# A causal convolution in front of a feed-forward layer: smaller TensorE tiles for the convolution, at another place in the block, and none of it on GpSimd

## The chip, the core and the metric

The kernel runs on one core of a Trainium2 chip. The metric is the time of one execution on the device in microseconds: the kernel before took 464.19 us (median of three runs, 463.25 to 464.36). The profile is one further execution of it, with a span of 462.7 us from the first to the last instruction; the granted TensorE clock was 1.000 throughout.

## What is computed

The input `x` has 8 sequences of 4160 tokens with 192 channels in float32. The 192 channels are 8 heads of 24. A softmax over `weight` (8 heads x 7 taps) gives seven convolution weights per head, and each channel is convolved causally along its sequence with the seven weights of its head. The 33,280 convolved tokens then pass through a maxout layer of width 768 with three branches, and a product that brings them back to 192 channels.

```python
out = np.einsum('hk,bskhg->bshg', w, x_unf)      # w = softmax(weight), 7 taps
h = np.maximum(np.maximum(x @ w1, x @ w2), x @ w3)
return (h @ w_out)
```

The kernel uses an identity to save a third of the maxout's work on the vector side. With `a = x(w1-w3)` and `b = x(w2-w3)`, the maximum of the three is `x w3 + max(relu(a), b)`. So only two products are made per token, the hidden value `max(relu(a), b)` goes through `w_out`, and the part `x w3 w_out` is one small product with the 192x192 matrix `m = w3 w_out`, worked out once at the start.

## The kernel before

**Blocks.** The tokens are cut into 65 blocks of 512. A loop over `t` runs the first product of block `t` (`l1`, L499) interleaved with the second product of block `t-1` (`st2`, L551). For each of the six groups `j` of 128 hidden features, `l1(t, j)` makes three pairs of matmuls with 512 columns each, and one call of `st2` makes five pairs with 192 columns each.

**Two lanes.** Every one of these matmuls contracts over 64 rows only. One half of the pair uses the lower 64 rows of the TensorE array (lane 0: the tiles `lp` and `po0`) and the other the upper 64 rows (lane 1: `lq`, `po1`), so the two run side by side. Both lanes need the convolved tokens in their own partitions, so the convolved block (`yd`) is kept twice, with the halves exchanged. After `l1`, ScalarE takes the ReLU of `lp` (L503) and VectorE the maximum with `lq` (L504).

**Three ways to convolve.** Blocks 0 to 3 are convolved at the start with the channels as outputs (`conv_dense`, L415). Twelve later blocks, those in `qpos`, are convolved on GpSimd: `load_q`, `cast_q`, a transposing DMA (`turn_q`), and then `tap_q`, seven multiplications (L229) with six additions (L237, L240). The other 49 are convolved on TensorE by `conv` (L397): block 4 alone, then 24 pairs of blocks. For this a block is cut into eight stretches of 64 tokens. Each is loaded with its six predecessors, which gives 70 rows, and multiplied with a banded 70x64 matrix that holds the seven taps of a head. One call of `conv` has 16 matmuls (8 heads, 2 column halves of the array), with 192 columns for a pair of blocks. The result `G` lies in four PSUM banks, two evacuated by ScalarE and two by VectorE (`evac`, L443).

**From `G` to `yd`.** A transposing DMA (`turn`, L454) brings the channels to the partitions, one DMA per block; two more DMAs (`double`, L462) write the exchanged copy. These, the loads of `x` (`load_x`, L144) and the stores of the result (`store`, L580) are all issued by SyncE's queue in the order of the program, and an issue that has to wait keeps those behind it waiting. GpSimd casts the loaded `x` to float16 (`cast_x`, L176).

**Where the convolution stands.** `conv` for block `t+3` and its successor is called right after `l1(t, 0)`, behind one single matmul of `st2` for lane 0 (`first_half_only`). The tiles of `l1` alternate between two banks for each lane (pools `psp` and `psq`), and `G` and the `po` tiles share four more (`psw`):

```python
l1(t, 0)
if t > 2 and u < NB:
    st2(t - 1, 0, NJ, True)
conv(u, PQ if t == 2 else WPWQ)
```

The order on each engine is that of the program text; nothing is reordered by a scheduler.

Of the kernel before, what the change touches and what calls it, by code (L numbers as in the profile page):

```python
# [14 lines left out]
P = 128  # L15
# [12 lines left out]
def kernel(  # L28
# [42 lines left out]
    qpos = [q for q in range(11, NB - 3, EVERY)] + [NB - 1]  # L71
# [23 lines left out]
    NR = NBLK // HALF  # L95

    def rows_of(t):
        rows = [(b, S + o) for (b, S, N, off) in blocks[t] for o in range(0, N, HALF)]
        assert len(rows) == NR
        return rows  # L100
# [4 lines left out]
    xfp = ctx.enter_context(tc.tile_pool(name="xfp", bufs=6))  # L105
# [5 lines left out]
    ydp = ctx.enter_context(tc.tile_pool(name="ydp", bufs=6))  # L111
# [9 lines left out]
    xin = {}  # L121

    def load_x(t, eng=nc.sync):
        if not 0 <= t < NB or t in qset:
            return
        pool, tag = (xfp, "xf") if t > 1 else ((xap, "xa"), (xbp, "xb"))[t]
        xf = pool.tile([P, NR, D], FP32, tag=tag, name=f"xf_{t}")
        if t < NDENSE:
            todo = [(0, c[3], c[1] * SEQ + c[2]) for c in chunks_of[t]]
        else:  # L130
            todo = [(PAD, HALF, b * SEQ) if s == 0 else (0, HALF + PAD, b * SEQ + s - PAD)
                    for b, s in rows_of(t)]
# [3 lines left out]
        while i < n:  # L136
            k = i
            while k + 1 < n and todo[k + 1][:2] == todo[i][:2] and row[k + 1] - row[k] == row[i + 1] - row[i]:
                k += 1
            step = row[i + 1] - row[i] if k > i else 0  # L140
            p0, rlen = todo[i][:2]
            src = bass.AP(tensor=x.tensor, offset=row[i] * D,
                          ap=[[D, rlen], [step * D, k - i + 1], [1, D]])
            eng.dma_start(out=xf[p0:p0 + rlen, i:k + 1, :], in_=src)  # L144
            if parts and parts[-1][0] == rlen:
                parts[-1] = (rlen, parts[-1][1], k + 1)
            else:
                parts.append((rlen, i, k + 1))
# [16 lines left out]
    def cast_x(t):  # L165
        if not 0 <= t < NB or t in qset:
            return
        xf, p0, _ = xin.pop(t)
        t0, u, nu = place(t)
        if u == 0:  # L170
            x16s[t0] = x16p.tile([P, NHEAD, 2, nu, NR // 2, GRP], FP16, tag="x16", name=f"x16_{t0}")
        if p0:
            nc.gpsimd.memset(xf[0:p0, 0, :], 0.0)
        K = HALF + PAD
        for c in range(2):
            nc.gpsimd.tensor_copy(out=x16s[t0][0:K, :, c, u, :, :].rearrange("p h r c -> p r h c"),  # L176
                                  in_=xf[0:K, c:NR:2, :].rearrange("p r (h c) -> p r h c", c=GRP))


# [41 lines left out]
    def tap_q(q, k):  # L221
# [17 lines left out]
        yd = dense[q] = ydp.tile([P, 2, NCH // 2, P], FP16, tag="yd", name=f"yd_{q}")  # L239
# [41 lines left out]
    for t in range(2, 7):  # L281
        load_x(t)

# [3 lines left out]
    nc.gpsimd.tensor_copy(out=ident16[:], in_=ident[:])  # L287
    idle = const.tile([P, NBLK], FP16)
# [25 lines left out]
    for v in range(2):  # L314
        nc.gpsimd.memset(xz[1][v][:], 0.0)
    wcol16 = const.tile([P, 3, KW], FP16)
# [70 lines left out]
    def conv(t, pools):  # L387
# [4 lines left out]
        per = NHEAD // n  # L392
        w = nu * (NR // 2) * GRP
        G = [pool.tile([P, per, w], FP32, tag=tag, name=f"G{i}_{t}") for i, (pool, tag) in enumerate(pools)]
        for h in range(NHEAD):
            for c in range(2):
                nc.tensor.matmul(  # L397
                    G[h // per][HALF * c:HALF * (c + 1), h % per, :],
                    lhsT=band[0:HALF + PAD, h, PAD:HALF + PAD],
                    rhs=x16s[t0][0:HALF + PAD, h, c, :, :, :].rearrange("p u r c -> p (u r c)"),  # L400
                    start=True, stop=True, tile_position=(0, HALF * c))
        slots[t0] = ysp.tile([P, nu, NR // 2, D], FP16, tag="ys", name=f"ys_{t}")
# [35 lines left out]
    def evac(t, i, copy=nc.scalar.copy):  # L438
# [3 lines left out]
        per = NHEAD // len(G)  # L442
        copy(out=slots[t][:, :, :, GRP * per * i:GRP * per * (i + 1)].rearrange(  # L443
# [3 lines left out]
    def turn(t):  # L447


        if t >= NB or t in qset:  # L450
            return
        t0, u, nu = place(t)
        yd = dense[t] = ydp.tile([P, 2, NCH // 2, P], FP16, tag="yd", name=f"yd_{t}")
        nc.sync.dma_start_transpose(out=yd[:, 0, :, :],  # L454
                                    in_=slots[t0][:, u, :, :].rearrange("p r d -> p (r d)"))

    def double(t):

        if NDENSE <= t < NB:
            yd = dense[t]  # L460
            for i in range(2):
                nc.sync.dma_start(out=yd[HALF * i:HALF * (i + 1), 1, :, :],  # L462
                                  in_=yd[HALF * (1 - i):HALF * (2 - i), 0, :, :])

    def spot(t, i, c, r):
# [3 lines left out]
        else:  # L469
            own, k = (NC * r + c) % 2, (NC * r + c) // 2  # L470
        return k + (0 if own == i else NCH // 2)

    def y_all(t, i, c):
        row = slice(HALF * i, HALF * (i + 1))
        if t < NDENSE:
            return dense[t][row, c, :]
        a = dense[t][row, 0, 0, :]
# [5 lines left out]
    def y_tok(t, i, c, s):  # L483
        row = slice(HALF * i, HALF * (i + 1))
        if t < NDENSE:
            return dense[t][row, c, P * s:P * (s + 1)]
        k = spot(t, i, c, s)
        return dense[t][row, k // 6, k % 6, :]

    def l1(t, j, pools=((psp, "p"), (psq, "q"))):  # L490


        N = blkN[t]
        ps = [pool.tile([P, NBLK], FP32, tag=tag, name=f"l{tag}{i}_{t}_{j}")
              for i, (pool, tag) in enumerate(pools)]
        for c in range(NC):
            for i in range(2):
                row = slice(HALF * i, HALF * (i + 1))
                nc.tensor.matmul(ps[i][:, 0:N], lhsT=wd[row, c, P * j:P * (j + 1)],  # L499
                                 rhs=y_all(t, i, c),  # L500
# [254 lines left out]
```

## Time and profile before

| | |
|---|---|
| time, median of 3 | 464.19 us |
| span of the profiled execution | 462.7 us |
| TensorE matmul busy | 454.4 us, 98% of the span |
| VectorE, ScalarE, GpSimd busy | 77%, 68%, 76% |
| bytes moved by DMA | 80.77 MB, mean 175 GB/s |
| `conv` calls on TensorE, matmuls in them | 25, 400 |
| blocks convolved on GpSimd | 12 |

The page of a profile begins with the busy time of each engine. Since matmuls are pipelined, a TensorE that is busy 98% of the time only says that some matmul was in flight, not that the array worked at its peak. What a stage costs is better read from the distance between the starts of its instructions in the timeline. The chain of waits is followed back from the last instruction; where it stays on one engine for hundreds of microseconds, that engine's queue set the end. In the rows for groups of instructions, `out<-in` gives the tiles, then come shape and count, the busy time, the mean duration of one, and the idle time of the engine just before them with what ended it. `64*128` means 64 rows and 128 columns of the array.

### The profile page before, as it was taken

What the parts mean: (1) busy time and instruction counts of PE and PEld (TensorE: products, weight loads), DVE (VectorE), ACT (ScalarE), POOL (GpSimd) and SP (SyncE); (2) the same over time, 40 slices, a digit from 0 to 9 for tenths busy, and PEclk for the clock granted to TensorE, in tenths of its full rate; (3) what the DMA queues carried; (4) which work ended last, traced back from release to release, by engine and by line L of the source; (5) the groups of instructions that cost most, each with busy time, mean ns of one, the idle gap of its engine ahead of it and who ended that gap; (6) DMA issues with size and microseconds to landing.
All of it is one profiled execution on the core that took longest, in us unless ns stands there. A gap on an engine that the chain in (4) does not pass through costs nothing.

```text
span 462.7 us, 17259 instructions
## 1 busy us (share of the span) xinstructions
PE 454.4 (98%) x6969; PEld 367.9 (80%) x6969; DVE 354.1 (77%) x595; ACT 314.3 (68%) x597; POOL 352.6 (76%) x501
## 2 busy tenths in 40 slices
PE   8999999999999999999999999999999999999997
PEld 4576788977877887888888888888888888888886
DVE  6777777777778787777878777777777777777775
ACT  5766566667676666767667676676767676676664
POOL 5753289999988978978967978978957969979500
PEclk9999999999999999999999999999999999999999
DMA  8959999999869878787789697698598797884423
GB/s 190 222 127 198 177 209 179 192 209 224 192 130 231 170 155 211 175 181 183 166 175 198 157 211 165 157 213 198 132 210 179 164 224 176 144 191 92 100 70 103
DMA packets 137527, 80.77 MB, mean 175 GB/s; under 512 B 58294, under 2 KB 137368, under 8 KB 137448
## 3 DMA queue, kind: packets, MB, share of 16 engines
q1 hardware_dynamic: 137176, 79.18, 79.1%
q8 instruction: 54, 0.88, 0.9%
q0 software_dynamic: 112, 0.39, 0.3%
q14 instruction: 25, 0.20, 0.2%
q10 hardware_dynamic: 160, 0.10, 0.1%
HBM read 29.85 MB, written 25.56 MB: 120 GB/s over the span
## 4 chain that ended last, share of the span: by engine, by line
PE 89%; POOL 5%; DMA 4%; issue 1%; DVE 0%; ACT 0%; POOLq 0%; DVEq 0%; SPq 0%
PE lq L499 35%; PE po L551 33%; PE lp L499 14%; PE G L397 4%; POOL tap L237 2%; POOL tap L229 2%; DMA yd<-ys 1%; PE idle L294 1%; DMA xt<-xq 1%; DMA yd<-yd 1%; PE D L415 1%; POOL x L176 1%; DMA xt<-xt 1%; PE lw L499 0%; PE band_cols L335 0%
## 5 line engine op out<-in xcount | busy, mean ns | idle before, releaser
L504 DVE TENSOR_TENSOR h<-r,lq 128x512 f16<-128x512 f16 x386 | 264.7, 686 | 99.5 <-ACT r L503 99.4
L503 ACT ACTIVATE r<-lp 128x512 f16<-128x512 f32 x386 | 230.5, 597 | 134.7 <-PE lp L499 123.8
L499 PE MATMUL lp<-yd,wd 64*128 64x512 f16 x1158 | 312.3, 376 | 2.2 <-DMA yd<-yd 1.6
L499 PE MATMUL lq<-yd,wd 64*128 64x512 f16 x1158 | 312.3, 376 | 0.3 <-DVE yd L431 0.3
L551 PE MATMUL po<-wo,h 64*128 64x192 f16 x3120 | 263.8, 243 | 0.7 <-issue 0.7
L551 PEld LDWEIGHTS <-h 64*128 64x128 f16 x3120 | 209.2, 94 | 22.2 <-issue 0.9
L499 PEld LDWEIGHTS <-wd 64*128 64x128 f16 x2340 | 160.9, 94 | 39.4 <-DMA yd<-yd 2.1
L176 POOL CAST x<-xf 70x768 f16<-70x768 f32 x98 | 77.8, 822 | 60.6 <-DMA xf<-in_x_dram 54.0
L229 POOL TENSOR_SCALAR tap<-xt,wcol 128x256 f32<-128x256 f16 x252 | 116.1, 478 | 3.9 <-DMA xt<-xt 3.3
L237 POOL TENSOR_TENSOR tap<-tap,tap 128x768 f32<-128x768 f32 x60 | 108.6, 1809 | 5.0
L551 PE MATMUL po<-m,yd 64*128 64x192 f16 x780 | 109.4, 243 | 0.0
L561 DVE TENSOR_TENSOR o<-a,po 128x384 f32<-128x384 f32 (+1 forms) x132 | 71.4, 541 | 1.2 <-ACT a L560 1.2
L551 PEld LDWEIGHTS <-yd 64*128 64x128 f16 x780 | 61.9, 94 | 11.8
L560 ACT COPY a<-po 128x384 f32<-128x384 f32 (+1 forms) x132 | 62.3, 473 | 3.0 <-PE po L551 3.0
L443 DVE CAST ys<-G 128x384 f16<-128x384 f32 x49 | 24.9, 550 | 0.6 <-PE G L397 0.6
L397 PEld LDWEIGHTS <-band 70*64 70x64 f16 x400 | 15.8, 109 | 9.9 <-PE lp L499 9.0
L240 POOL TENSOR_TENSOR yd<-tap,tap 128x768 f16<-128x768 f32 x12 | 21.8, 1814 | 1.0
L397 PE MATMUL G<-x,band 70*64 70x192 f16 (+1 forms) x400 | 21.2, 248 | 0.7 <-POOL x L176 0.5
L443 ACT CAST ys<-G 128x384 f16<-128x384 f32 x49 | 21.0, 484 | 0.8 <-PE G L397 0.8
L198 POOL CAST xq<-xl 128x384 f16<-128x384 f32 x24 | 11.4, 505 | 0.0
L256 POOL CAST xz<-xf 112x80 f16<-112x80 f32 (+2 forms) x18 | 5.2, 330 | 4.5 <-DMA xf<-in_x_dram 4.5
L294 PE MATMUL idle<-idle 128*128 128x512 f16 x15 | 6.4, 573 | 1.2 <-DVE idle L289 1.2
(52 smaller groups left out, 68.6 us busy)
## 6 DMA issues: line engine op xcount, KB each, us to landing
out_dram<-o SPq DMA_DIRECT2D x61, 384.0 KB
xf<-in_x_dram SPq DMA_DIRECT2D x47, 420.0 KB
yd<-yd SPq DMA_DIRECT2D x122, 96.0 KB
xl<-in_x_dram SPq DMA_DIRECT2D x12, 384.0 KB
xf<-in_x_dram SPq DMA_DIRECT2D x5, 367.5 KB
ws<-in_moe_w_dram SPq DMA_DIRECT2D x6, 192.0 KB
out_dram<-o SPq DMA_DIRECT2D x5, 192.0 KB
yd<-ys SPq DMA_TRANSPOSE x49
```

The lines of the kernel that those rows point to most:

```text
L176: nc.gpsimd.tensor_copy(out=x16s[t0][0:K, :, c, u, :, :].rearrange("p h r c -> p r h c"), in_=xf[0:K, c:NR:2, :].rearrange("p r (h c) -> p ...
L229: nc.gpsimd.tensor_scalar(out=part[:, 2 * c:2 * c + 2, :], in0=xt[:, 2 * c:2 * c + 2, LEAD - PAD + k:LEAD - PAD + k + P], scalar1=wcol[:, ...
L237: nc.gpsimd.tensor_add(out=accs[q][:], in0=accs[q][:], in1=part[:])
L240: nc.gpsimd.tensor_add(out=yd[:, 0, :, :], in0=accs.pop(q)[:], in1=part[:])
L397: nc.tensor.matmul(G[h // per][HALF * c:HALF * (c + 1), h % per, :], lhsT=band[0:HALF + PAD, h, PAD:HALF + PAD], rhs=x16s[t0][0:HALF + PAD ...
L443: copy(out=slots[t][:, :, :, GRP * per * i:GRP * per * (i + 1)].rearrange("p u r (h c) -> p h (u r) c", c=GRP), in_=G[i][:].rearrange("p h ...
L499: nc.tensor.matmul(ps[i][:, 0:N], lhsT=wd[row, c, P * j:P * (j + 1)], rhs=y_all(t, i, c), start=(c == 0), stop=(c == NC - 1))
L503: nc.scalar.activation(out=r[:, 0:N], in_=ps[0][:, 0:N], func=AF.Relu)
L504: nc.vector.tensor_max(out=hs[t][:, j, 0:N], in0=r[:, 0:N], in1=ps[1][:, 0:N])
L551: nc.tensor.matmul(ps[b0, i][:, s % 2, :], lhsT=a, rhs=b, start=first, stop=last)
L560: nc.scalar.copy(out=a[:, ss, :], in_=ps[s0, 0][:, ss, :])
L561: nc.vector.tensor_add(out=outs[t][:, s0:s + 1, :], in0=a[:, ss, :], in1=ps[s0, 1][:, ss, :])
```

## The change

The change has five parts.

1. **Smaller convolution tiles.** A stretch is 32 tokens instead of 64, loaded with seven predecessors: 39 rows, of which the first meets a zero in the band. Eight stretches lie in partitions 0 to 38 and eight in 64 to 102. A call of `conv` then has 64 matmuls of 39 rows, 32 output columns and 96 streamed columns (for a pair), which address eight tiles of the array: two row halves by four column quarters. `G` still has four banks, each now belonging to one row half.
2. **No GpSimd blocks.** `qpos` is empty. All blocks from 4 on are convolved on TensorE: 31 calls of `conv`, one for block 4 and one for each of 30 pairs.
3. **Another place.** `conv` stands behind `l1(t, 1)` and eight matmuls of `st2` for lane 1, twelve for lane 0 (`OWN`, `AHEAD`). From then on lane 1 is four matmuls behind. The order of the two lanes is worked out by a small queue (`mm`, `op`, `emit`) that counts streamed columns for each lane; `meet` empties it.
4. **Transposes by pair.** `turn` transposes both blocks of a pair with two DMAs, one per row half, and `double` writes the exchanged copy for both blocks at once. The number of bytes for each block stays the same.
5. **Queues.** The stores of the result are issued by GpSimd instead of SyncE, except for the last blocks. Six input buffers are kept for the whole run, and GpSimd clears partitions 32 to 63 of each once, so that the rows between the two halves hold zeros; the load fills 32 to 38 afterwards.

Smaller tiles let the same array work on eight pieces of the convolution at once, and the place behind the second tile is meant to give the banks that the convolution needs time to come free.

```diff
-    qpos = [q for q in range(11, NB - 3, EVERY)] + [NB - 1]
+    qpos = []
...
-    NR = NBLK // HALF
+    TOK = 32
+    NR = NBLK // TOK // 2
+    LAP = PAD + 1
+    KR = TOK + LAP
...
-            todo = [(PAD, HALF, b * SEQ) if s == 0 else (0, HALF + PAD, b * SEQ + s - PAD)
-                    for b, s in rows_of(t)]
+            todo = [(HALF * (i // NR) + (0 if s else LAP), KR if s else TOK,
+                     b * SEQ + s - (LAP if s else 0), i % NR) for i, (b, s) in enumerate(rows_of(t))]
...
         for h in range(NHEAD):
-            for c in range(2):
-                nc.tensor.matmul(
-                    G[h // per][HALF * c:HALF * (c + 1), h % per, :],
-                    lhsT=band[0:HALF + PAD, h, PAD:HALF + PAD],
-                    rhs=x16s[t0][0:HALF + PAD, h, c, :, :, :].rearrange("p u r c -> p (u r c)"),
-                    start=True, stop=True, tile_position=(0, HALF * c))
+            for j in range(4):
+                for i in range(2):
+                    row = slice(HALF * i, HALF * i + KR)
+                    nc.tensor.matmul(
+                        G[2 * (h // per) + i][TOK * j:TOK * (j + 1), h % per, :],
+                        lhsT=band[row, h, HALF * i + LAP:HALF * i + KR],
+                        rhs=x16s[t0][row, h, j, :, :, :].rearrange("p u r c -> p (u r c)"),
+                        start=True, stop=True, tile_position=(HALF * i, TOK * j))
...
+        for i in range(2):
+            nc.sync.dma_start_transpose(out=yp[:, 0, i, :, :, :].rearrange("p u k n -> p (u k) n"),
+                                        in_=slots[t][:, i, :, :, :].rearrange("p u r d -> p (u r d)"))
...
+    EVEN = [5, 10, 15, 20, 25, 30]
+    ROOM = [5, 13, 17, 21, 26, 30]
+    OWN, AHEAD = 3, 4
...
         for j in range(1, NJ):
             l1(t, j)
-            st2(t - 1, j, NJ)
+            if late and j == 1:
+                st2(t - 1, (cuts[0] + OWN + AHEAD, cuts[0] + OWN))
+                meet()
+                conv(u, WPWQ)
+                for i in (0, 2):
+                    evac(u, i)
+                for i in (1, 3):
+                    evac(u, i, nc.vector.tensor_copy)
+                turn(u)
+            st2(t - 1, (cuts[j], cuts[j]))
...
-            store(t - 2, 0, 4, (nc.sync,))
+            op(lambda t=t: store(t - 2, 0, 4, (nc.gpsimd,)))
```

## The prediction

> **What bounds the kernel now.** I read the page's busy times, then the chain of waits, then the timeline around one convolution. The chain, in order of time, shows the rhythm: the convolutions of the steady stretch repeat exactly.
>
> ```profile
> 114.57 0.85 PE G L397 x16
> ...
> 148.33 0.85 PE G L397 x16
> ```
>
> Five blocks with two convolutions take 148.33 - 114.57 = 33.76 us. A block without one is read from the timeline, from the starts of the first `lp` matmul of successive `j`:
>
> ```profile
> 99.86 0.38 PE L499 MATMUL lp<-yd,wd 64*128 64x512 f16 x1
> ...
> 100.92 0.38 PE L499 MATMUL lp<-yd,wd 64*128 64x512 f16 x1
> ...
> 101.98 0.38 PE L499 MATMUL lp<-yd,wd 64*128 64x512 f16 x1
> ```
>
> One `j` is 1.06 us, six are 6.36 us. Consecutive `lp` inside a `j` start 0.21 to 0.22 us apart, so three fill 0.65 us and five `po` the remaining 0.41 us (0.082 each): nothing is left over, TensorE is full. So a convolution costs (33.76 - 5 x 6.36) / 2 = **0.98 us** of TensorE time. Where these go:
>
> ```profile
> 114.27 0.38 PE L499 MATMUL lq<-yd,wd 64*128 64x512 f16 x1
> 114.28 0.24 PE L551 MATMUL po<-m,yd 64*128 64x192 f16 x1
> 114.57 0.85 PE L397 MATMUL G<-x,band 70*64 70x192 f16 x16
> 115.35 0.26 PE L551 MATMUL po<-m,yd 64*128 64x192 f16 x2
> ```
>
> The 16 matmuls are eight bursts of two (both column halves). First to last start is 0.85 less one duration of 0.25, in seven steps: 0.086 each, 0.69 for eight. The last `lq` would be followed after 0.22, at 114.49, and the convolution starts at 114.57: 0.08 lost on entry, and about 0.09 on exit (last burst at 115.17 + 0.09, next `po` at 115.35). Lane 0 ran dry at 114.28 + 0.08 = 114.36, 0.12 before lane 1. The sum is 0.69 + 0.17 + 0.12 = 0.98.
>
> All other engines wait for TensorE: in the table of waits the first two rows are ScalarE on `lp` and VectorE on ScalarE, and TensorE's own waits for others are small and at the start:
>
> ```profile
> ACT r L503 <- PE lp L499: 123.8, 253, 1.3
> DVE h L504 <- ACT r L503: 99.6, 259, 1.3
> ...
> PEld L499 <- DMA yd<-yd: 2.1, 2, 1.2
> ```
>
> **What the skill says.** "TensorEngine Tiling", section Key Properties: "Changing tiling mode (not just tile) drains the TensorE". The trace agrees: 0.08 and 0.09 us at each change. "TensorE: Matmul & The Clock Gate", Part 3, says that a weight load overlaps with running matmuls only when its row group differs; the trace of `conv_dense`, where four column tiles share all rows, does not show that cost (below). The same part gives 6.32x for nine tiles packed by row and column; no run here shows such packing yet. "DMA: Bandwidth & Descriptors", Issuing engines are not separate DMA queues: moving stores to another issuing engine saves only issue time, the same 16 engines move the bytes.
>
> **The change, part by part.**
>
> *Conv tiles.* No row shows eight tiles. The nearest are the column-tiled stretches at the start:
>
> ```profile
> 28.33 1.09 PE L415 MATMUL D<-band,xz 112*32 112x103 f16 x60
> 29.36 0.53 PE L397 MATMUL G<-x,band 70*64 70x96 f16 x16
> ```
>
> The first is 60 matmuls with 60 weight loads, by the code ten bursts of four tiles and ten of two: (1.09 - 0.21) / 19 = 0.046 us a burst, whether it has two or four tiles. The second, 96 columns, has eight bursts: (0.53 - 0.21) / 7 = 0.046. At 0.217 us for 512 columns, 103 and 96 columns stream in 0.044 and 0.041. So a burst costs its columns, and the tiles in it are free. The new call is eight bursts (heads) of eight tiles with 96 columns. If the eight run together: 8 x 0.046 = 0.37 us. From above: if the two row halves take turns, 16 x 0.046 = 0.74. I take 0.37, because `l1` shows that the two row halves run independently (`lp` and `lq` overlap all the time) and `conv_dense` that the column quarters do.
>
> *Place.* Entry and exit still change the mode: 0.17. The new order counts columns for each lane, and lane 0's lead of four is exactly lane 1's backlog since the last `meet`, so both lanes should run dry together: I put 0.03 for the rest instead of 0.12. A call becomes 0.37 + 0.17 + 0.03 = **0.57 us**. The lag leaves one lane idle for four `po` before the first and after the last call: 4 x 0.082 = 0.3 once.
>
> *Count.* Out go 24 calls for pairs, 24 x 0.98 = 23.5. In come 30 x 0.57 = 17.1. Block 4's call stays about the same (0.53 with the tail, before; half the columns after). **Net -6.4 us.**
>
> *GpSimd.* It loses the taps (116.1 + 108.6 + 21.8 us) and gains 24 casts at 0.82 and some 60 stores at 0.93 (the one such issue in the trace). It goes from 353 to some 180 us busy and bounds nothing: 0. A store queued behind a cast that waits for its load is late, but three output buffers hide that. The memsets (32x1536 float32, an estimate of 1.4 us each from 0.87 us for half the bytes) lie in idle time: GpSimd waits 2.68 us for the first load.
>
> *Evacuation and banks.* Six more calls, same shapes. In a block with a call VectorE has six maxima 0.61 apart, two additions 0.46 apart and two evacuations in 1.02: 5.6 us of 6.9. A bank of `G` is wanted again after one `lp` and some `po`, about a microsecond later. Hidden, but the tightest point: from 0 to 0.15 us a call.
>
> *DMA.* Loads grow from 49 x 420 + 12 x 384 KB to 61 x 468 KB, +3.3 of 80.8 MB; the share in the steady stretch is 0.83, so 0.86 to 0.87: hidden.
>
> *The start.* Here nothing is far ahead, and the DMA share is 0.96 between 45 and 82 us. Before, `turn(4)` is issued at 32.71 and the double behind it at 38.96, so a transpose took some 6 us to land; `l1(4)` waited 1.15 us, `l1(5)` 0.92. After, block 5 needs the transposes of its whole pair, SyncE has them behind the doubles of block 4 and two loads, and the convolution comes 2 us later in block 3. From 40 us: doubles 1.1, loads 1.1, two transposes 3.6 (before: two took 3.62 to issue), 4 to 5 to land, double 4 to 5: 54 to 56, against 52.5 before and 51 wanted. Without the GpSimd blocks' loads the DMA is freer. I take **+2.5**, bounds 0 and +5.
>
> Sum: 464.2 - 6.4 + 0.3 + 2.5 = **460.6 us**.
>
> **Rivals.**
> - *The row halves take turns* (or issue limits the rate): a call is 0.74 + 0.20 = 0.94, 30 calls 28.2, so +4.7 + 2.8: **471.7**, slower. For it: no trace shows both packings together. Against: both show alone. Chance 0.10.
> - *The gain is given back in waits*: start +5, banks 0.15 x 30 = 4.5: 464.2 - 6.4 + 0.3 + 9.5 = **467.6**, slower. For it: the long chain from `G` to `yd` in one SyncE queue; against: after the start there are some 10 us of slack, and VectorE has a fifth of its time free. Chance 0.11.
> - *More than forecast*: the start costs nothing and one of the two drains vanishes, since the row split stays: -6.4 - 30 x 0.09 + 0.3 = -8.8: **455.4**. Chance 0.15.
> - The forecast: 0.64, between 457.5 and 463.
>
> **Numbers.** Faster is the forecast and the third rival, less the forecast's upper edge: 0.77. Same 0.05, slower 0.18. The range leaves out the first rival and a little at the bottom: 455 to 468.
>
> **What would show it.** A `G` group of 64 in about 0.37 + 0.21 us by the timeline, and two conv blocks apart by 2 x 6.36 + 0.57 = 13.3 us. The chain stays on TensorE. Idle of `lp` or its weight load on the doubled block near 44 and 51 us gives the start's cost. Wrong would be: `G` stretched to 0.9, `lp` or `po` behind a convolution waiting for ScalarE or VectorE, or casts holding `G` in every block.

## The result, and the profile after

The kernel after the change takes 468.56 us (median of four runs, 467.81 to 469.06), the kernel before took 463.82 us in the same comparison: a ratio of 1.0101, interval 1.0081 to 1.0121. It is 4.7 us slower; the prediction said 3.6 us faster. The profiled execution has a span of 466.0 us against 462.7 before. The first 60 us differ from one execution to the next by some microseconds (in several profiles the granted clock was half there for 3 to 7 us), the distance of two blocks in the steady stretch does not.

Two parts of the page of the kernel after, the busy times and the chain that ended last:

```profile
PE 455.3 (98%) x8553; PEld 421.2 (90%) x8553; DVE 363.1 (78%) x607; ACT 319.2 (68%) x609; POOL 167.7 (36%) x232
...
PE 94%; DMA 3%; DVE 1%; issue 1%; SPq 0%; ACT 0%; DVEq 0%
```

GpSimd fell from 76% to 36%, as forecast, and the end is still set by TensorE. So no other engine became the bound: TensorE itself needs as long as before. The chain of waits, cut to the steady stretch, shows where (start, duration):

```profile
104.05 0.68 PE G L419 x64
117.55 0.68 PE G L419 x64
131.06 0.68 PE G L419 x64
```

From call to call it is 13.50 or 13.51 us. Two blocks without a convolution are 2 x 6.36 = 12.72 us, so one call costs 0.78 to 0.79 us (**0.78** in what follows). The forecast was 0.57 (and 13.3 us for two blocks), the call before cost 0.98. With 0.78 the sum of the count is 30 x 0.78 - 24 x 0.98 = -0.1 us in place of -6.4, that is, nothing: a call became a fifth cheaper, and there are a quarter more of them.

Its timeline around one call, which answers to the four lines of the kernel before at 114.27 (first the last matmul before it, last the first behind it):

```profile
103.80 0.24 PE L627 MATMUL po<-m,yp 64*128 64x192 f16 x1
103.97 0.75 PE L419 MATMUL G<-x,band 39*32 39x96 f16 x64
104.66 0.25 PE L627 MATMUL po<-wo,h 64*128 64x192 f16 x1
```

The last `po` would be followed after 0.08, at 103.88; the call starts 0.09 later. TensorE is back at its products at 104.66, and it does not wait there for another engine. In the table of waits (us in total, times, longest) the two rows that the prediction showed first are still there, and TensorE's own waits for the doubled copies, one each for blocks 4 and 5, are 2.0 us together:

```profile
ACT r L577 <- PE lp L570: 112.7, 255, 2.1
DVE h L578 <- ACT r L577: 92.9, 257, 1.3
...
PE lp L570 <- DMA yp<-yp: 1.1, 1, 1.1
...
PE lq L570 <- DMA yp<-yp: 0.9, 1, 0.9
```

The same waits of TensorE's matmuls in the kernel before were 1.6 us:

```profile
PE lp L499 <- DMA yd<-yd: 1.6, 2, 0.9
```

These 0.4 us belong to the start. In the steady stretch no such wait is left, so the time there is in the call itself.

What a call spends its time on is seen when one counts its matmuls up to a moment. This is the table by stretches of the kernel after, for the matmuls and weight loads of L419 alone, in four stretches that all begin shortly before that call and end later and later (stretch, length, busy us and number of matmuls, the same for weight loads, clock, DMA share, GB/s):

```profile
103.90:104.14 0.24, 0.17 (x32) 0.17 (x33) 1.00 0.82 134
103.90:104.21 0.31, 0.23 (x32) 0.24 (x33) 1.00 0.84 141
103.90:104.37 0.47, 0.40 (x51) 0.39 (x51) 1.00 0.83 154
103.90:104.53 0.63, 0.56 (x64) 0.55 (x64) 1.00 0.85 174
```

The first matmul starts at 103.975. By 104.14 half of the call has been started: 32 matmuls in 0.16 us, bursts of eight 0.042 apart, inside a burst 3.3 ns from one to the next. Then nothing starts until 104.215. Then 19 start in 0.155 us and 13 more in the next 0.16: the single records are 8.3 ns apart, one by one, with no bursts, and the last two follow 34 ns apart. First to last start is 0.55 us; with 0.09 on entry, 0.04 for the last burst and 0.09 on exit this is 0.78.

At the start, the timeline of VectorE and GpSimd in the kernel after (start, duration, operation, and in brackets the idle time before with what ended it):

```profile
4.36 4.17 DVE L276 CAST xz<-xf 112x240 f16<-112x240 f32 x3 [1.20 <-DMA xf<-in_x_dram]
```

```profile
4.48 0.87 POOL L276 CAST xz<-xf 112x80 f16<-112x80 f32 x3
5.30 1.74 POOL L334 MEMSET xz<- 128x960 f16 x2
7.09 1.37 POOL L141 MEMSET xf<- 32x1536 f32 x1
```

The same three casts on VectorE took 2.87 us before:

```profile
4.32 2.87 DVE L256 CAST xz<-xf 112x240 f16<-112x240 f32 x3 [1.18 <-DMA xf<-in_x_dram]
```

Now they end at 8.53, just after GpSimd's last clear (8.46). By the single records it is the third cast that grew, from 0.18 us to 1.47. L141 is the clearing that the change added; the first convolution waits behind it, which the timeline of TensorE shows at the next matmul:

```profile
8.57 1.82 PE L437 MATMUL D<-band,xz 112*32 112x103 f16 x58 [1.08 <-DVE xz L276]
```

Before, these matmuls went on from 7.22 without a break. From the starts of the blocks in the two timelines, the kernel after is behind by 1.80 us at block 2, 1.97 at block 7, 0.85 at block 10 (the kernel before lost about 0.9 there in a wait for a cast on GpSimd), 2.30 at block 64 and 3.34 at the end. In the steady stretch the two are best compared ten blocks apart, where the kernel before has made four calls and the kernel after five: 1.47 at block 14, 1.48 at 24, 2.07 at 34, 2.09 at 44, 2.11 at 54. But for half a microsecond in block 29, which is taken up below, five new calls cost what four old ones did.

### The profile page after: what moved, and what is told of

Same layout as the page of the kernel before. It is cut to its first block, busy times and chain, and to the rows that moved or that the text cites. A ratio compares the mean times of both kernels' runs of the same rounds, so it can differ in the third digit from the quotient of the medians.

```text
span 466.0 us, 20154 instructions
## 1 busy us (share of the span) xinstructions
PE 455.3 (98%) x8553; PEld 421.2 (90%) x8553; DVE 363.1 (78%) x607; ACT 319.2 (68%) x609; POOL 167.7 (36%) x232
## 4 chain that ended last, share of the span: by engine, by line
PE 94%; DMA 3%; DVE 1%; issue 1%; SPq 0%; ACT 0%; DVEq 0%
PE po L627 35%; PE lq L570 30%; PE lp L570 22%; PE G L419 4%; PE D L437 1%; DMA yp<-yp 1%; DVE xz L276 1%; DMA yp<-ys 1%; DMA xf<-in_x_dram 1%; PE lw L570 0%; PE idle L313 0%; DVE h L578 0%; PE pm L400 0%; ACT r L577 0%; PE pm L396 0%
## 5 line engine op out<-in xcount | busy, mean ns | idle before, releaser
L627 PE MATMUL po<-wo,h 64*128 64x192 f16 x3120 | 336.2, 243 | 0.3 <-issue 0.3
L570 PE MATMUL lp<-yp,wd 64*128 64x512 f16 x1098 | 295.8, 376 | 1.2 <-DMA yp<-yp 1.1
L570 PE MATMUL lq<-yp,wd 64*128 64x512 f16 x1098 | 295.6, 376 | 0.9 <-DMA yp<-yp 0.9
L627 PEld LDWEIGHTS <-h 64*128 64x128 f16 x3120 | 245.8, 94 | 5.1
L198 POOL CAST x<-xf 103x768 f16<-103x768 f32 x122 | 97.5, 831 | 249.5 <-DMA xf<-in_x_dram 145.3
L627 PE MATMUL po<-m,yp 64*128 64x192 f16 x732 | 143.3, 243 | 0.0
L627 PEld LDWEIGHTS <-yp 64*128 64x128 f16 x732 | 67.3, 94 | 0.6
L666 POOL DMA_DIRECT2D out_dram<-o x63 | 47.3, 751 | 28.2 <-DVE o L636 27.8
L419 PEld LDWEIGHTS <-band 39*32 39x32 f16 x1984 | 18.6, 91 | 5.1 <-issue 4.7
L419 PE MATMUL G<-x,band 39*32 39x96 f16 (+1 forms) x1984 | 23.2, 207 | 0.0
L570 PE MATMUL lp<-yd,wd 64*128 64x512 f16 x60 | 17.2, 389 | 1.7 <-DVE yd L453 1.7
L570 PE MATMUL lq<-yd,wd 64*128 64x512 f16 x60 | 17.1, 389 | 0.2 <-DVE h L578 0.2
L141 POOL MEMSET xf<- 32x1536 f32 x6 | 8.2, 1369 | 0.3
```

The lines of the kernel that those rows point to most:

```text
L141: nc.gpsimd.memset(xf[TOK:HALF, :, :], 0.0)
L198: nc.gpsimd.tensor_copy(out=x16s[t0][0:K, :, :, u, r, :].rearrange("p h j c -> p j h c"), in_=xf[0:K, 4 * r:4 * r + 4, :].rearrange("p j ( ...
L419: nc.tensor.matmul(G[2 * (h // per) + i][TOK * j:TOK * (j + 1), h % per, :], lhsT=band[row, h, HALF * i + LAP:HALF * i + KR], rhs=x16s[t0] ...
L570: nc.tensor.matmul(ps[i][:], lhsT=wd[HALF * i:HALF * (i + 1), c, P * j:P * (j + 1)], rhs=y_all(t, i, c), start=(c == 0), stop=(c == NC - 1))
L627: nc.tensor.matmul(ps[b0, i][:, s % 2, :], lhsT=a, rhs=b, start=first, stop=last)
L666: qs[0].dma_start(out=bass.AP(tensor=out.tensor, offset=r * D, ap=[[D, n], [step * D, s1 - s0], [1, D]]), in_=ob[p0:p0 + n, s0:s1, :])
```

## The experiments

Each compares with runs of the kernel before on the same chip; edits are against the kernel after unless said otherwise. Beside the time I give the distance of two blocks in the steady stretch.

**What makes a call cost 0.78.** The first theory is that the second half of a call is limited by the number of its instructions; the rivals are the columns, the banks and the place.

*wide32*: half as many matmuls with twice the columns (both heads of a pair get the band of the even one, so the weights of the odd heads are left out).

```diff
-        for h in range(NHEAD):
+        for h in range(0, NHEAD, 2):
...
-                        G[2 * (h // per) + i][TOK * j:TOK * (j + 1), h % per, :],
+                        G[2 * (h // per) + i][TOK * j:TOK * (j + 1), h % per:h % per + 2, :],
...
-                        rhs=x16s[t0][row, h, j, :, :, :].rearrange("p u r c -> p (u r c)"),
+                        rhs=x16s[t0][row, h:h + 2, j, :, :, :].rearrange("p h u r c -> p h (u r c)"),
```

> The kernel after with half as many convolution matmuls: for each pair of heads one matmul streams 192 columns with the band of the even head, so the odd heads get the wrong weights; columns streamed by each of the eight tiles, banks, evacuation and transposes are unchanged. Theory 1 (a call of 64 weight loads and 64 matmuls outruns the supply of instructions: the first 32 pairs start 3.3 ns apart, the other 32 pairs 8.3 ns apart after a gap of 0.08 us): 32 pairs all come at the fast rate, four bursts of 0.082 us = 0.33 us instead of about 0.55, a call costs 0.55 to 0.57 instead of 0.78 us, 30 calls save 6 to 6.6 us: 462 to 462.6 us. Theory 2 (the array is the limit in the second half: row halves or banks collide): the same columns take the same time, 468.5 us. Theory 3 (the second half waits for the two banks of G2 and G3): unchanged, 468.5 us, with the gap still in the middle.

Measured: 463.42 us, ratio 0.9974 (0.9949 to 0.9998). Its chain of waits:

```profile
105.97 0.45 PE G L419 x32
119.26 0.45 PE G L419 x32
```

13.29 us for two blocks: a call costs 0.57. The same columns pass through the same tiles, in half as many instructions, and 13.51 - 13.29 = 0.22 us a call is gone. The time is just above the forecast (462 to 462.6). All 32 pairs run 3 to 4 ns apart inside their burst; first to last start is 0.28.

*narrow*: all 64 matmuls, each with 24 columns in place of 96 (three quarters of the convolution are left out).

```diff
-                        rhs=x16s[t0][row, h, j, :, :, :].rearrange("p u r c -> p (u r c)"),
+                        rhs=x16s[t0][row, h, j, 0, 0, :],
```

> The kernel after with all 64 weight loads and matmuls of a convolution call, but each streams 24 columns instead of 96; the evacuation copies these over the place of the columns left out, so three quarters of the convolution are not computed. Theory 1 (supply of instructions): the first half shrinks at most from 0.16 to 0.11 us (32 pairs at 3.3 ns), the restart and the 32 pairs at 8.3 ns stay: 0 to 0.08 us less a call, 466 to 468.6 us. Theory 2 (array rate): three quarters of 0.55 us go, some 0.35 us a call, 457 to 459 us.

Measured: 467.47 us, ratio 1.0076 (1.0058 to 1.0095), 13.45 us for two blocks. The count inside a call, as above:

```profile
105.70:105.87 0.17, 0.12 (x32) 0.12 (x33) 1.00 1.01 158
105.70:105.95 0.25, 0.20 (x32) 0.20 (x33) 1.00 1.00 141
105.70:106.11 0.41, 0.36 (x51) 0.35 (x51) 1.00 0.99 131
105.70:106.27 0.57, 0.52 (x64) 0.51 (x64) 1.00 0.98 128
```

The first half became shorter (0.12 us instead of 0.16, from 105.748), since there the columns count. The second half did not: again 19 matmuls in 0.15 us and 13 in the next 0.16, 8.3 ns apart but for the last two, 0.31 us from its first to its last start in both kernels. A quarter of the columns saves only 0.06 us a call, so in the second half the array is not the limit. The kernel after has a third width of its own: its call for block 4 alone, 48 columns, breaks off after 32 pairs too (for 0.097 us) and goes on 8.3 ns apart.

*splitstart*: every call cut in two, heads 0 to 3 behind `l1(t, 1)` and heads 4 to 7 behind `l1(t, 2)`, on top of *start* (below).

```diff
-                conv(u, WPWQ)
+                conv(u, WPWQ, 0)
...
+            if late and j == 2:
+                st2(t - 1, (cuts[2], cuts[2] - AHEAD))
+                meet()
+                conv(u, WPWQ, 1)
```

> start with every call of conv cut in two: heads 0 to 3 behind l1(t, 1), heads 4 to 7 behind l1(t, 2), 32 matmuls and 32 weight loads each, with an own change of the tiling each. Theory (64 instructions are queued ahead and run fast, the rest come at 4.2 ns an instruction): both halves run at 3 to 4 ns a pair, first to last start about 0.17 us each; a half call costs 0.17 for the drains and 0.18 to 0.25 for the rest, two of them 0.75 to 0.85, so the time is within 2 us of start's 467.5. Rival (the second 32 pairs are slow for another reason, such as the banks of heads 4 to 7): the second half still takes 8 ns a pair, and the extra drains make 31 x 0.17 = 5 us: 472 us.

Measured: 486.39 us, ratio 1.0454 (1.0407 to 1.0501). As a forecast of the time this missed by 19 us, as a test of the halves it is clear. The count in the two half calls of one block:

```profile
151.55:151.71 0.16, 0.08 (x16) 0.08 (x24) 1.00 0.91 192
151.55:151.79 0.24, 0.16 (x32) 0.16 (x32) 1.00 0.92 198
152.95:153.09 0.14, 0.09 (x16) 0.09 (x24) 1.00 1.40 293
152.95:153.17 0.22, 0.17 (x32) 0.17 (x32) 1.00 1.21 253
```

Both halves now run at the fast rate: 32 matmuls within 0.16 us, the same heads 4 to 7 that need 0.31 in the second half of a whole call. So it is neither their bands nor their banks; it is that 64 instructions (32 weight loads and 32 matmuls) stand before them without a pause. With 0.04 for its last burst a fast half takes 0.20 us, two of them 0.41; the prediction had 0.37 for the whole call, which in one piece takes 0.59. The time was lost behind the second half, in the timeline of TensorE:

```profile
154.15 0.37 PE L573 MATMUL lq<-yp,wd 64*128 64x512 f16 x1 [0.25 <-DVE h L581]
```

Lane 1's next product starts 0.62 us after lane 0's second one, since of lane 1's two banks one holds `G` until VectorE has evacuated it (from 154.01 on) and the other is freed by the maximum that ends at 154.10; two blocks take 14.10 us. My expectation had only counted drains there.

*quad*: the saving of *wide32* with nothing left out. On top of *start*, from block 21 on, four blocks are cast together and a call takes four heads for all of them: 32 matmuls with 192 columns, still one call every two blocks. Loads and casts must run four blocks further ahead, and with them only two buffers of casted inputs are kept instead of three.

```diff
-                        rhs=x16s[t0][row, h, j, :, :, :].rearrange("p u r c -> p (u r c)"),
+                        rhs=x16s[t0][row, h0 + h, j, 0:nu, :, :].rearrange("p u r c -> p (u r c)"),
...
-            load_x(t + 6)
+        while t > 3 and loaded[0] <= t + 6 + ahead(t, (9, 11, 13, 14)):
+            load_x(loaded[0])
+            loaded[0] += 1
```

> start with the same convolution cut otherwise, nothing left out: from block 21 on, four blocks are cast together, and a call of conv takes four of the eight heads for all four blocks: 32 matmuls with 192 columns instead of 64 with 96. There is still one call every two blocks; loads and casts run four blocks further ahead, transposes and doubles stay where they are. Theory (the second 32 pairs of a call are held by the supply of instructions): as in wide32 a call costs about 0.56 us instead of 0.78, two blocks 13.28 us instead of 13.51 from block 21 on; 22 such calls take 4.8 us from start's 467.5: 462.7 us, between 461 and 464.5, faster than before the change. Rival (what wide32 saved came from the columns and the work that it left out, or the deeper loads hold the transposes back): the period stays at 13.5 or waits of lp for the doubled copy appear: 467 us or more.

Measured: 474.3 us, ratio 1.0213 (1.0155 to 1.0272). The chain of waits in its later part:

```profile
302.93 0.46 PE G L428 x32
316.22 0.45 PE G L428 x32
```

13.29 us, as forecast, in a complete kernel. But it was 12.5 us behind *start* at block 17, before the first such call: it lost 4.7 us by block 5, with longer waits for the doubled copies and 6.8 us at half the granted clock, and 3.8 and 3.9 us in blocks 13 and 15, where further loads and casts are squeezed in. There TensorE stood still for 1.9 and 2.1 us, by the profile for nothing that it shows (`issue`), and each time 3.4 us at half the granted clock followed (0.50 from 119.2 to 122.4 and from 136.3 to 139.5). From block 19 on it gained 0.22 us every two blocks.

*quad2* starts at block 25 and spreads the further loads over blocks 10 to 18:

```diff
+    QUAD0 = 25
...
+        while t > 3 and loaded[0] <= t + 6 + ahead(t, (10, 12, 14, 16, 18)):
```

> quad with another run-up: the calls for four blocks begin at block 25 instead of 21, the loads get ahead by one block every two blocks from block 10 on, each further cast stands at the end of its block and two blocks behind its load, and the casted inputs keep three buffers as in start. Theory: the stalls of quad (2.2 us each in blocks 13 and 15) came from casts for which GpSimd had to wait while stores stood behind them, so they are gone; 20 calls at 0.56 instead of 0.78 take 4.4 us from start's 467.5: 463.1 us, between 461.5 and 465, with two blocks in 13.29 us from block 25 on. Rival (the deeper loads meet a full DMA whenever they are made): stalls of 1 us or more come back in blocks 10 to 20, 466 us or more.

Measured: 479.39 us, ratio 1.0322 (1.0285 to 1.0359). What the rival forecast came: stalls of 0.3 to 2.3 us returned in blocks 11 to 21, several in the middle of a convolution. That a full DMA makes them, as the rival has it, is not shown: the two longest are again `issue`. The forecast had blamed the order of casts alone.

*quad3* needs only three further loads (blocks 10, 13, 16), has the two calls in consecutive blocks, and four output buffers:

```diff
+        while t > 3 and loaded[0] <= t + 6 + ahead(t, (10, 13, 16)):
...
-    outp = ctx.enter_context(tc.tile_pool(name="outp", bufs=3))
+    outp = ctx.enter_context(tc.tile_pool(name="outp", bufs=4))
```

> quad2 with the two calls for four blocks in consecutive blocks (four and three blocks ahead), so that only three more loads have to be made ahead, one every three blocks from block 10, each further cast one block behind its load, and with four output buffers instead of three. Theory (quad2's stalls of 1 to 2.5 us in blocks 12 to 21 came from too many loads in a short stretch and from stores that held VectorE's output buffers): no stall over 0.6 us after block 9; 20 calls at 0.56 instead of 0.78 take 4.4 us from start's 467.5: 463 us, between 461 and 466. Rival (any load ahead of the present ones meets the full DMA, or two calls in consecutive blocks are too much for VectorE): stalls of 1 us or more come back after block 9 and the time is 467 us or more.

Measured: 470.26 us, ratio 1.0134 (1.0101 to 1.0167). Its chain, over four blocks with two calls:

```profile
305.79 0.46 PE G L428 x32
312.71 0.46 PE G L428 x32
332.36 0.45 PE G L428 x32
```

332.36 - 305.79 = 26.57 us, less 4 x 6.36 is 1.13, so 0.565 a call even in consecutive blocks. Against *start* in the same four-block rhythm (2 x 13.51 = 27.02) that is 0.22 a call again. But stalls of 1.1 and 2.6 us came back, as the rival had said; against *start* it lost 2.9 us by block 6 and 6.3 us in blocks 15 to 21. None of the three beats the kernel before: where they are past the run-up they are the fastest complete kernels here, and the run-up costs more than 20 calls bring.

**The start.** *start* moves the third clearing and the load of block 6 behind the cast of `w_out`:

```diff
-    load_x(6)
...
     nc.gpsimd.tensor_copy(out=wo[:], in_=wos[:])
+    load_x(6)
```

> The kernel after with one edit at the start: the load of block 6, and with it the clearing of its buffer on GpSimd (1.37 us), is issued after the cast of w_out instead of ahead of the first convolutions. Theory 1 (VectorE's casts of the first block, 4.17 us instead of 2.87, are held until GpSimd's run of memsets ends, and the shift makes two more copies collide with a GpSimd subtraction): the first convolution starts at 7.2 instead of 8.6 us, block 2 starts 1.3 to 1.9 us earlier, 466.7 to 467.2 us. Rival (the casts are slow because the loads land late or the DMA is busy): no change, 468.5 us.

Measured: 467.46 us (466.05 to 470.64), ratio 1.0091 (1.0067 to 1.0116). VectorE's three casts are back at 2.88 us, and block 2 starts at 26.88 instead of 29.37. The cause of the delay is shown. Little of the gain is left at the end: the medians lie 1.1 us apart, and the intervals of the ratios overlap. Most of it went into waits of blocks 4 and 5 for their doubled copies, in the timeline of TensorE:

```profile
44.56 0.37 PE L569 MATMUL lp<-yp,wd 64*128 64x512 f16 x1 [1.86 <-DMA yp<-yp]
...
53.24 0.37 PE L569 MATMUL lp<-yp,wd 64*128 64x512 f16 x1 [1.35 <-DMA yp<-yp]
```

In the kernel before these two waits were 0.93 and 0.69 us. So two limits lie one behind the other, and taking the first away uncovers the second: in the profiles 2.5 us gained at block 2 are 0.9 at block 7.

*early5* also calls the convolution of blocks 5 and 6 in block 2:

```diff
-    convs_at = {2: 4, 3: 5, 4: 7}
+    convs_at = {2: 4, 4: 7}
...
+            if t == 2 and j == 3:
+                st2(1, (22, 18))
+                meet()
+                conv(5, WPWQ)
```

> The edit of 'start' and one more: the convolution of blocks 5 and 6 is called in block 2 (behind its fourth product tile) instead of block 3, so that its transposes are issued some 5 us earlier. In 'start', TensorE waits 2.4 us for the exchanged copy of block 4 and 2.3 us for that of block 5. Theory 1 (after the start is mended, the chain from G by transposes and exchanged copies through one queue is what holds blocks 4 and 5): the wait of block 5 goes, that of block 4 stays, about 2 us less than 'start': 465.5 us. Rival (the DMA engines are full there, so earlier transposes only land as late): same as 'start', 467.5 us.

Measured: 468.14 us, ratio 1.0073 (1.005 to 1.0096). The gain did not come. Block 5's wait is gone, but block 4's grew from 1.86 to 3.39 us, since the transposes of blocks 5 and 6 now stand before the doubling of block 4. The timeline of SyncE's queue shows it (DMA issues and how long each held the queue):

```profile
41.77 2.60 SPq L479 DMA_TRANSPOSE yp<-ys  x2
44.47 1.87 SPq L492 DMA_DIRECT2D yp<-yp  x2
```

**The other parts, one at a time.** *noq* is the kernel before without GpSimd blocks, so that 31 old calls stand where there were 25:

```diff
-    qpos = [q for q in range(11, NB - 3, EVERY)] + [NB - 1]
+    qpos = []
```

> The kernel before with one part of the change: no GpSimd convolution, so 31 calls of the old convolution with 70x64 tiles instead of 25; its place, the stores and the transposes stay as before. Theory 1 (the new call saves 0.98 - 0.78 = 0.2 us, and six more calls at 0.98 would cost 5.9): 463.8 + 5.9 - about 0.9 for block 9, which waited for GpSimd before = 468 to 470 us, so that the new tiles did earn back what the six calls cost. Rival (leaving GpSimd out costs nothing since its engine and the DMA get freer): 463 to 465 us, and the new tiles would be the loss.

Measured: 467.85 us, ratio 1.0105 (1.0082 to 1.0127); block 64 starts 5.8 us later than before (the profile is of the slowest of its four runs, 470.34). Six more old calls would be 6 x 0.98 = 5.9. So leaving GpSimd costs what the calls cost, and what remains for the new tiles is to earn that back, which at 0.2 a call they just do.

*ahead0* takes lane 0's lead of four matmuls away:

```diff
-    OWN, AHEAD = 3, 4
+    OWN, AHEAD = 3, 0
```

> The kernel after without lane 0's lead: eight matmuls of the second product for each lane ahead of a convolution, so no lane lags. Theory A (the lead only shifts the lanes; VectorE and ScalarE have time): 0.3 us less at the two ends, same time otherwise, 468.3 us. Theory B (without the lag, the ReLU of lane 0's tile and the maximum with lane 1's become due at once, and the banks that the convolution and the tile behind it need come free later): TensorE waits behind convolutions for ScalarE or VectorE, some 0.1 to 0.3 us a call, 472 to 478 us.

Measured: 478.56 us, ratio 1.029 (1.0242 to 1.0337); two blocks take some 13.76 us, 0.26 more a call. Three product tiles behind the convolution the timeline shows lane 1 (`lq`) starting 0.26 us behind lane 0, held back by a bank that VectorE's maximum has emptied only at 207.20:

```profile
206.99 0.38 PE L570 MATMUL lp<-yp,wd 64*128 64x512 f16 x1
...
207.25 0.37 PE L570 MATMUL lq<-yp,wd 64*128 64x512 f16 x1
```

So at the new place the lead is worth a quarter of a microsecond a call. The prediction had counted only that both lanes run dry together, 0.09. What the place by itself is worth was not tried.

*startsync* is *start* with the stores on SyncE's queue as before the change:

```diff
-            op(lambda t=t: store(t - 2, 0, 4, (nc.gpsimd,)))
+            op(lambda t=t: store(t - 2, 0, 4, (nc.sync,)))
```

> start with one difference: the stores are issued by SyncE instead of GpSimd. Theory: without GpSimd blocks the queue of the stores does not matter, the time stays within 0.5 us of start's 467.5 and the period of two blocks stays 13.5 us. Rival (a part of the 0.78 us a call is a wait that the move of the stores brought): the period falls towards 13.3 us and the time to about 464.

Measured: 479.15 us (472.9 to 480.18), ratio 1.0251 (1.0161 to 1.0341). Both theories fell: the medians are 11.7 us apart, with a wide spread. The chain of waits of *startsync* by line:

```profile
by line: PE po L626 21.1%; PE lq L569 17.5%; DMA yp<-ys 15.0%; PE lp L569 11.4%; DMA out_dram<-o 8.2%; DMA xf<-in_x_dram 4.6%; DMA yp<-yp 4.6%; SPq L492 3.0%; PE G L418 2.6%; SPq L166 2.6%; issue 1.9%; DMA w3s<-in_moe_w_dram 1.2%; DVE h L57
```

Transposes and stores, which were on no chain in the steady stretch, now hold 23% of it. In its table of waits `PEld L569 <- DMA yp<-yp` has 9.7 us in 16 waits. The prediction had said that this move "saves only issue time". The Trainium skill, "DMA: Bandwidth & Descriptors", section Issuing engines are not separate DMA queues, says that another issuing engine saves issue time, usually little; here it made 11.7 us. The bytes are the same, and they moved at 183 GB/s between 100 and 400 us in *startsync* and 190 in *start*. Whether it is the order in SyncE's queue that costs, or that GpSimd's stores go by another DMA queue (`q0`, 17% of the 16 engines' time between 100 and 400 us in *start*, absent in *startsync*), was not separated.

*mixed10* is *start* with ten GpSimd blocks (26 calls); *best* is *mixed10* with *early5*'s place; *mixsync* is *mixed10* with the stores on SyncE; *beforeq* is the kernel before with the stores on GpSimd.

```diff
-    qpos = []
+    qpos = list(range(21, NB - 3, EVERY)) + [NB - 1]
```

> The edit of 'start', and ten blocks convolved on GpSimd again, as the kernel before had it for twelve (here blocks 21, 26 and so on to 61, and 64): 26 calls of the new convolution instead of 31. Theory 1 (a call costs TensorE 0.78 us, GpSimd's taps lie beside): five calls less, 467.5 - 3.9 = 463.6 us. Rival (GpSimd's taps slow the casts, stores and the other engines through shared memory ports, or the GpSimd queue holds back stores and casts): 465.5 us or more, with TensorE waiting for casts.

> The edits of 'early5' and 'mixed10' together. If each is worth what was said and they don't meet (one is at the start, the other from block 16 on): 467.5 - 2.0 - 3.9 = 461.6 us, less than the kernel before at 463.7. Rival (with the start mended, block 4 holds the rest, and GpSimd's casts collide with taps): 463 to 464 us.

> Ten blocks on GpSimd as in mixed10 (26 calls of conv instead of 31), the early start of the casts as in start, but the stores are issued by SyncE as before the change. Theory (stores queued behind the taps in GpSimd's queue made mixed10's stalls): VectorE no longer waits for stores, five calls less at 0.78 us take 3.9 us from start's 467.5: about 463.5 us, between 461 and 465. Rival (the casts behind the taps are enough to stall conv): still 470 us or more, with waits of conv's matmuls for the cast in blocks that follow the taps.

> The kernel before with one difference: the stores are issued by GpSimd instead of SyncE. Theory (an in-order queue hurts whatever stands behind a waiting instruction): with 12 GpSimd blocks the stores stand behind taps and casts, VectorE's additions wait for an output buffer as in mixed10: slower by 3 to 10 us, 467 to 474. Rival (SyncE's queue was a hidden bound before too, as in startsync): transposes and loads come earlier, the waits of blocks 4 and 5 and of the steady stretch shrink: 463 us or less.

Measured: *mixed10* 477.48 us, ratio 1.0268 (1.0196 to 1.0339); *best* 475.28, 1.0214 (1.0157 to 1.0271); *mixsync* 484.98, 1.0422 (1.038 to 1.0464); *beforeq* 469.31, 1.0105 (1.0072 to 1.0137). Only *beforeq* came out as its theory had it. *mixed10* and *mixsync* went the way of their rivals, and *best* is 11 us above both of its forecasts. Rows of the table of waits of *mixed10* (us in total, times, longest):

```profile
DVE o L635 <- DMA out_dram<-o: 5.8, 5, 1.7
...
PE G L418 <- POOL x L198: 4.1, 3, 2.1
```

Stores and casts stand behind the taps in GpSimd's queue: an output buffer is not free, so VectorE's addition waits, so TensorE's bank is not free; or the casted input is late. In *mixsync* VectorE's waits for stores shrank to 0.9 us, but TensorE's for casted inputs grew:

```profile
PE G L418 <- POOL x L198: 13.3, 8, 3.2
```

Before the longest of these GpSimd had stood idle for some 6 us until the load landed, so there it was not the taps that held the cast back. *beforeq* was 2.1 us ahead at block 5 and lost 6.8 us in block 9: a convolution waited for casts behind the taps until 82.4 us, and 6.8 us at half the granted clock followed. Its steady stretch is that of the kernel before (33.76 us for five blocks).

So the place of the stores has no value of its own. With the rest of the change GpSimd is better, without taps (467.46 against 479.15) and with them (477.48 against 484.98); in the kernel before SyncE is better (463.95 against 469.31). It is not the taps that decide this. Which other part of the change does is not shown.

## Why the prediction was wrong, step by step

- **The step that failed: "a burst costs its columns, and the tiles in it are free", 0.37 us for a call's bursts.** It was taken from two rows of the kernel before, and neither could show the limit. The 60 matmuls of `D` with their 60 weight loads took 0.88 us from first to last start, 7.4 ns an instruction; the 16 of a call of a single block with their weight loads 0.32 us, 10 ns; even the bursts of four tiles, 8 instructions in 0.046 us, are 5.8 ns each. The new call asks for 16 instructions in each burst of 0.046 us, 2.9 ns each, faster than either row kept up. For the first 64 instructions that is so: 3.3 ns a pair inside a burst, and the array rate of 0.042 a burst, so the eight tiles do run together. After them come a pause of 0.08 and pairs at 8.3 ns, 0.067 for eight. So the term of 0.37 measured 0.59 (0.55 from first to last start and 0.04 for the last burst). The call as a whole was mis-sized by 0.78 - 0.57 = 0.21 us, 6.3 us over 30 calls, nearly the whole net gain. That the number of instructions in a row sets it is shown by *wide32*, *narrow*, *splitstart* and *quad*; weight loads and matmuls always changed together, so which of the two counts is not separated. That the 64 are those which had queued up while TensorE streamed 512-column products, and 4.2 ns an instruction is the rate at which new ones arrive, is my reading of it, and it doesn't explain the last two pairs, 34 ns apart; the Trainium skill, "TensorE: Matmul & The Clock Gate", section Architectural detail: the array is 16× 32×32, not 1× 128×128, gives TensorE's queue a depth of 64, which agrees with the number at which the rate breaks.
- **The first rival had it in a bracket**: "or issue limits the rate". It got 0.10, and was priced as if all bursts took twice as long (0.94). The truth lies between, half a call at each rate. For a packing that no row shows, the room between 0.57 and 0.94 should have had more weight than its two ends; at 0.78 the sum is no gain.
- **The entry, the exit and the lanes**: right. 0.09 and 0.09 at the change of the tiling, and both lanes run dry at the same time (103.798 and 103.802 for the last `po` of each). The lead also does what the prediction left out (*ahead0*).
- **The start, +2.5**: that the size came out (1.97 us at block 8) is luck, the step was wrong. It was argued from transposes and doubles of block 5; these brought some 0.4 us more waiting, while 1.80 us had been lost by block 2. The clearing of `xf`, which the prediction put "in idle time", was in idle time of GpSimd, but not of VectorE: the cast on VectorE ended only after it, 4.17 us instead of 2.87. (The 1.4 us for a clear came out, 1.37, but from a misreading: the clear of 0.87 us that it was scaled from has 960 elements in each partition against 1536, not half the bytes.) The Trainium skill, "SBUF — State Buffer", section SBUF: two separate sides, says that the two engines share a port pair, and that GpSimd or a VectorE operation in a mode with two ports holds it for a whole instruction while the other is blocked; the trace agrees, with 1.3 us for a clear of 1.37. That this cast runs in such a mode no run here shows.
- **Stores through GpSimd, 0**: not a term that can be had alone. In the kernel before the move costs 5.4 us (*beforeq*), with the rest of the change it saves 11.7 (*startsync*). That no such term was missed in the sum is luck.
- **DMA and evacuation hidden**: right in the kernel after (no wait of TensorE for it between 100 and 400 us), though the DMA share was 0.90 to 0.97 there, against 0.82 to 0.86 before and a forecast of 0.86 to 0.87. In *quad* it was 1.01 between 100 and 200 us.
- **The end**: 1.0 us more from block 64 to the end in place of 0.3. With lane 1's lag the last matmul starts 0.27 us later, but the last store is issued only 0.05 us later than before, counted from block 64; nearly all of the 1.0 us lies between that issue and the end.

With the measured call the prediction's own sum is 464.2 - 0.1 + 0.3 + 2.5 = 466.9. What is missing to 468.56 is the rest of the end (0.7), some 0.4 that I can't place, and a stall of about half a microsecond in block 29, in which TensorE waited for nothing that the profile shows (its chain has `220.14 0.34 issue`); *start* does not have it. That stall is left open, and so is why the old kernel's stores did no harm on SyncE's queue while those of *startsync* do; the transposes by pair were not tried apart.

## What to carry to other kernels

When many small matmuls replace few large ones, count instructions beside columns: here a burst of tiles was only free for the first 64 instructions of a call, and the same product cut along another axis (half as many matmuls with twice the columns) can win the time of the rest back. A part that seems to cost nothing by the busy shares can carry the rest of a change or ruin it: ask which in-order queue it leaves and which it joins, what waits there, and try it with the rest of the change in place. And before deeper prefetching buys a cheaper stage, reckon what its run-up costs.

## What the runs showed of the hardware

- Pairs of a weight load and a matmul of 39x32 tiles start 3.3 ns apart inside bursts of eight for the first 64 instructions after large products. Then, after 0.08 to 0.10 us, they start 8.3 ns apart, with 96 columns, 48 and 24 alike; with 96 and 24 the last two come 34 ns apart.
- Eight tiles (two row halves, four column quarters) stream together: 0.042 us for a burst of eight with 96 columns.
- A change between 64x128 and 39x32 tiles costs 0.09 us each way, and every half call of *splitstart* pays it again.
- A clear of 32x1536 float32 on GpSimd (1.37 us) kept a cast of VectorE from ending: 1.47 us instead of 0.18, and 4.17 instead of 2.87 for the three in a row.
- In *quad* two stalls of TensorE of about 2 us were each followed by 3.4 us at half the granted clock, and their blocks lost 3.8 to 3.9 us; stalls of 2.3 us in *quad2* were not followed by it.
- A kernel that computes the same can move by 12 us with the engine that issues its stores, at the same bytes and nearly the same rate (183 and 190 GB/s), and another by 5 us the other way.
